# Float64 weights converted a pair of blocks at a time: operations of 512 columns in place of 256

## The chip, the cores and the metric

The kernel runs on one core of one Trainium2 chip. The metric is the device time of one execution in microseconds (us). A core has five engines with queues of their own: TensorE (PE, matrix products), VectorE (DVE), ScalarE (ACT), GpSimd (POOL), and SyncE (SP), which here issues most of the DMAs.

## The reference

A layer that mixes channels in the frequency domain, and two gated MLPs on its result; the weights of the MLPs come as float64, because NumPy's scaling of them made them so.

```python
X = np.fft.rfft(x, axis=1)                  # x: 2 x 3008 x 256, float32
Yr = Xr @ w_r - Xi @ w_i + b_r
Yi = Xr @ w_i + Xi @ w_r + b_i
Yr = np.sign(Yr) * np.maximum(np.abs(Yr) - 0.01, 0.0)      # Yi likewise
y = np.fft.irfft(Y, n=3008, axis=1)
...
h = x @ w_in                                # x: 6016 x 256, w_in: 256 x 2048
x = (h * sigmoid(1.702 * h)) @ w_out        # w_out: 2048 x 256
h = x @ w_in2
out = (h * sigmoid(h)) @ w_out2
```

## The kernel before

The program goes through a forward transform as matrix products (0 to about 77 us), the channel mixing (to about 152 us), the inverse transform (to about 216 us), and the two MLPs. The tokens of an MLP are worked on in six blocks, `i` = 0 to 5, of 1024 tokens (the last has 896). A block has eight groups, `p` = 0 to 7, one for each pair of 128-wide blocks of the hidden width. A group makes the seven products of a Strassen-Winograd scheme with `w_in` (L772), adds them up (L784 on DVE, L794 on ACT), applies the activation (L776), splits its result in an upper and a lower float32 part (L778 on ACT, L780 on DVE or POOL), and multiplies with `w_out` (L744). One group is 45 matmuls. Layer 0 lasts from 216 to about 748 us, layer 1 from there on.

**The conversion.** Each of the 64 blocks of the four weight matrices (two layers, `w_in` and `w_out`, 16 blocks each) is 128 x 256 float64. `cv_load` brings it in by one DMA on SP (L146, 256 KB, tile `raw64`). ACT takes the magnitude of the upper words (L155, tile `cv_c`), and DVE makes five steps: two operations with a constant (L160, L161), one that joins the sign to it (L162, writes `cv_a`), another with a constant (L163), and one that makes the rest of the value from the lower words (L164, writes `cv_c`). `settle` then adds the two parts (L221, by the table `cva` three times in four on POOL and else on DVE). For layer 1, and for the first blocks of `w_out`, the sum is spilled to DRAM (L224) and fetched later; else it is put in place. The five steps are laid into the list `fill`, from which `pump` takes them between the MLP's adds (L785), so that they are spread over DVE's queue.

**Placing.** `place_out` makes the upper part of a block by a copy on ACT (L99) and the lower by a subtraction (L100). `place_in` waits for two blocks, makes four sums of 128 columns from them on DVE (L195, L196, L198, L200), and splits the seven left factors in four pieces: of 256, 128, 256 and 256 columns, each with a copy (L99) and a subtraction (L100, on DVE or POOL by the tables `pil` and `mvl`).

**Buffers.** The pool `cv` has two `raw64` buffers, two `cv_c`, four `cv_a` and two for fetched blocks of `w_out`, each of one block, and one of 512 columns for the sums.

**What sets the order.** Ahead of the MLP, `tick` converts a block after those groups that the tables `tf` (forward), `tm` (mixing) and `ti` (inverse) list, 19 blocks in all; in block 0 the table `kb` gives the blocks converted in each group, 16 in all; after that `kr` = 1 block a group is converted up to the last, which is started at about 609 us. Inside a group, `settle` runs at hook 1 and `window`, which starts the next blocks, at hook 2. A scheduler orders the engines' queues by a simulated timeline, but `region` keeps some of them in the order of the program: POOL and SP in the forward part, SP in the mixing, PE in the inverse, none in block 0 of layer 0, and DVE and SP in its later blocks.

## Time and profile before

| | |
|---|---|
| Three runs | 1244.52, 1243.29, 1242.84 us; median 1243.29 us |
| Span of the profiled execution | 1241.9 us, 1.4 us below that median |
| Busy: PE, DVE, ACT, POOL | 1193.9, 904.3, 709.1, 691.3 us |
| DVE's steps L160 to L164 | 64 of each, 30 of each between 80 and 318 us |

The profiled execution's own time is given by its span alone. Busy times are sums of durations; the durations of neighbouring instructions of DVE overlap a little, so that the distance from start to start is shorter than the duration. A busy PE is not PE at its peak, since matmuls are pipelined and their ends are modelled; the number of matmuls in a stretch says more.

### The profile page before, as it was taken

The page shows a single profiled execution, that of the slowest core. Times are in us where ns is not written, and L with a number is a line of the kernel's source. Part 1 is how long each engine was busy: PE and PEld are TensorE (multiplying, and loading weights), DVE is VectorE, ACT ScalarE, POOL GpSimd, SP SyncE. Part 2 cuts the span into 40 slices and gives each one's busy share as a digit, 9 for nine tenths or more (in the row PEclk, how much of TensorE's full clock was granted, in tenths as well). Part 3 has the DMA queues.
Part 4 walks back from the last instruction along what each step waited for, and adds up shares of the span by engine and source line. Part 5 has one row for each costly group of instructions (what it writes and reads, how often), then busy time and mean ns, then how long its engine had stood idle before and what let it go on. Part 6 is the DMA issues. An engine that isn't in the chain of part 4 may idle for free.

```text
span 1241.9 us, 15776 instructions
## 1 busy us (share of the span) xinstructions
PE 1193.9 (96%) x5220; PEld 969.5 (78%) x5220; DVE 904.3 (73%) x1543; ACT 709.1 (57%) x1393; POOL 691.3 (56%) x579
## 2 busy tenths in 40 slices
PE   7889889799999999999999999999999999999998
PEld 4877679577688787787888977888888888888897
DVE  7899999999967868678758886465564564655654
ACT  3566644656655656556556675565564555554654
POOL 4666655646545647547556575464464554553643
PEclk9889889799999999999999999999999999999999
DMA  8441123111110111111100110000000000000000
GB/s 330 170 160 55 52 73 130 36 52 60 33 44 27 39 39 39 39 39 38 43 18 9 56 39 9 1 35 1 1 34 1 1 35 1 27 8 1 35 1 30
DMA packets 33012, 57.11 MB, mean 46 GB/s; under 512 B 3233, under 2 KB 22689, under 8 KB 31650
## 3 DMA queue, kind: packets, MB, share of 16 engines
q1 hardware_dynamic: 30882, 41.42, 10.3%
q0 software_dynamic: 2048, 14.68, 3.2%
q8 instruction: 41, 0.67, 0.2%
q14 instruction: 41, 0.34, 0.1%
HBM read 44.68 MB, written 11.40 MB: 45 GB/s over the span
## 4 chain that ended last, share of the span: by engine, by line
PE 65%; DVE 7%; issue 2%; ACT 1%; POOL 0%; DMA 0%; DVEq 0%; ACTq 0%
PE o L744 35%; PE x L772 30%; DVE yt L784 3%; DVE cv_s L196 1%; DVE tmp L697 1%; DVE g L780 0%; DVE x L100 0%; ACT yt L776 0%; DMA raw<-in_wo 0%; DVE tmp L691 0%; ACT g L778 0%; ACT wi L99 0%; DVE cv_c L164 0%; ACT x L99 0%; DVE wi L100 0%
## 5 line engine op out<-in xcount | busy, mean ns | idle before, releaser
L784 DVE TENSOR_TENSOR yt<-yt,x 128x512 f32<-128x512 f32 (+1 forms) x672 | 450.9, 673 | 275.2 <-PE x L772 204.8
L780 POOL TENSOR_TENSOR g<-yt,g 128x512 fp32r<-128x512 f32 (+1 forms) x324 | 416.4, 1295 | 418.1 <-ACT g L778 301.2
L744 PE MATMUL o<-g,wo 128*128 128x512 f32 (+1 forms) x2304 | 604.3, 392 | 2.4 <-ACT yt L748 1.1
L772 PE MATMUL x<-x,wi 128*128 128x512 f32 (+1 forms) x2016 | 543.3, 394 | 15.2 <-DVE yt L784 10.8
L744 PEld LDWEIGHTS o<-g,wo 128*128 128x128 f32 x2304 | 432.9, 188 | 101.7 <-ACT g L778 2.8
L772 PEld LDWEIGHTS x<-x,wi 128*128 128x128 f32 x2016 | 378.4, 189 | 108.3 <-DVE yt L784 19.6
L776 ACT ACTIVATE yt<-yt 128x512 f32<-128x512 f32 (+1 forms) x384 | 237.4, 622 | 292.0 <-DVE yt L784 290.0
L778 ACT CAST g<-yt 128x512 fp32r<-128x512 f32 (+1 forms) x384 | 231.9, 609 | 8.6
L780 DVE TENSOR_TENSOR g<-yt,g 128x512 fp32r<-128x512 f32 (+1 forms) x60 | 49.0, 819 | 33.1 <-ACT g L778 33.1
L100 POOL TENSOR_TENSOR x<-yt,x 128x512 fp32r<-128x512 f32 (+1 forms) x41 | 58.5, 1435 | 14.5 <-ACT x L99 12.7
L155 ACT ACTIVATE cv_c<-raw 128x256 f32<-128x256 f32 x64 | 27.8, 438 | 65.6 <-DMA raw<-in_wo 36.6
L794 ACT COPY yt<-x 128x512 f32<-128x512 f32 (+1 forms) x96 | 54.9, 572 | 9.9 <-PE x L772 9.5
L221 POOL TENSOR_TENSOR cv_a<-cv_a,cv_c 128x256 f32<-128x256 f32 x48 | 41.2, 863 | 23.9 <-DVE cv_c L164 21.4
L164 DVE SCALAR_TENSOR_TENSOR cv_c<-raw,cv_c 128x256 f32<-128x256 uint32 x64 | 51.0, 805 | 0.0
L356 PE MATMUL psi<-m,fh 128*128 128x376 f32 (+3 forms) x208 | 48.7, 324 | 0.3 <-ACT rt L623 0.3
L496 PE MATMUL psm<-wc_hi,xtl 128*128 128x512 f32 x96 | 39.3, 413 | 3.3 <-DVE xtl L100 3.3
L356 PE MATMUL psf<-m,xh 128*128 128x376 f32 (+1 forms) x160 | 39.3, 341 | 2.0 <-ACT xh L307 1.2
L496 PE MATMUL psm<-wc_hi,xth 128*128 128x512 f32 x96 | 40.2, 419 | 1.0 <-ACT xth L99 1.0
L356 PE MATMUL psi<-m,fl 128*128 128x376 f32 (+3 forms) x104 | 34.2, 329 | 6.8 <-POOL fl L100 5.0
L496 PE MATMUL psm<-wc_lo,xth 128*128 128x512 f32 x96 | 39.0, 406 | 0.0
L356 PEld LDWEIGHTS psi<-m,fh 128*128 128x128 f32 x208 | 37.1, 196 | 0.5 <-ACT rt L623 0.4
L356 PEld LDWEIGHTS psf<-m,xh 128*128 128x128 f32 x160 | 30.3, 216 | 3.3 <-ACT xh L307 1.7
(111 smaller groups left out, 979.6 us busy)
## 6 DMA issues: line engine op xcount, KB each, us to landing
raw<-in_wi SPq DMA_DIRECT2D x32, 256.0 KB, 2.7
raw<-in_wo SPq DMA_DIRECT2D x32, 256.0 KB, 2.7
raw<-in_x SPq DMA_DIRECT2D x12, 512.0 KB, 4.9
out_t<-yt SPq DMA_DIRECT2D x20, 256.0 KB, 2.0
m<-in_mf POOLq DMA_DIRECT2D x4, 1128.0 KB, 7.9
m<-in_mi POOLq DMA_DIRECT2D x4, 1128.0 KB, 6.2
w_out<-cv_a SPq DMA_DIRECT2D x24, 128.0 KB, 1.7
cv_ld<-w_out SPq DMA_DIRECT2D x24, 128.0 KB, 2.0
```

The source lines that it names most:

```text
L100: (lo_eng or nc.vector).tensor_sub(lo, src, r32(hi))
L164: lambda: stt(out=c, in0=w[:, :, 0], scalar=2.0**-52, in1=c, op0=ALU.mult, op1=ALU.mult),
L221: E('cva', u[2]).tensor_add(a, a, c)
L356: nc.tensor.matmul(ps, a, z, start=i == 0 and x == 0, stop=i == last and x == 2)
L496: nc.tensor.matmul(t, a, w, start=(n == 0), stop=(n == 11 and grp == 1))
L744: nc.tensor.matmul(acc[h, mm], st, mv, start=first and k == 0, stop=last and k == 2)
L772: nc.tensor.matmul(ps, st, mv, start=m == 0, stop=m == 2)
L776: nc.scalar.activation(g, g, func)
L778: nc.scalar.copy(gh, g)
L780: E('gl3' if l else 'gl0' if i == 0 else 'gl2' if i == last else 'gl', ng[0]).tensor_sub(gl, g, r32(gh))
L784: (nc.vector.tensor_sub if sub else nc.vector.tensor_add)(out, u, v)
L794: nc.scalar.copy(ya, p1)
```

## The change

Every list, buffer and step of the conversion goes by pairs of blocks. A pair is loaded as 128 x 512 float64 (512 KB): of `w_out` by one DMA (L149 of the changed kernel), of `w_in` by two of 256 KB (L145, L146), which lay the four pieces in the order that the placing wants. ACT's magnitude (L158), the five steps (L163 to L167) and the add (L218) have 512 columns, and one spill or fetch moves 256 KB. `place_out` is one copy and one subtraction of 512 columns for a pair; `place_in` keeps its four sums of 128 columns and splits in two pieces, of 384 and 512 columns. The MLP's own lines move up by four (L784 is L780, L780 is L776).

The pool has one `raw64` and one `cv_c` buffer, two `cv_a` and one for fetched pairs of `w_out`, each of a pair; their bytes are the same. A pair's load can start when L167 of the pair ahead has read `raw64`, and its magnitude when that pair's add has read `cv_c`. The tables `cva`, `pil` and `mvl` are now read by the number of the pair. Ahead of the MLP nine pairs are converted (three by `tf`, three by `tm`, three by `ti`), in block 0 nine (one a group, and by the new table `kb2` a second one in group 1, at hooks 4 and 5), and one in each of the next 14 groups, those of block 1 and the first six of block 2.

```diff
-CFG = {..., 'tf': [6, 9, 12], 'tm': [2, 3, 4, 5, 7, 14], 'ti': [2, 2, 3, 4, 5, 10, 12, 13, 13, 15, 15], 'kb': [2, 4, 2, 2, 2, 2, 0, 2], ...}
+CFG = {..., 'tf': [6, 9, 12], 'tm': [2, 4, 7], 'ti': [2, 5, 13], 'kb': [1, 1, 1, 1, 1, 1, 1, 1], ...}
...
-            raw = cv_p.tile([P, CU], mybir.dt.int64, tag="raw", name="raw64")
+            raw = cv_p.tile([P, 2 * CU], mybir.dt.int64, tag="raw", name="raw64", bufs=1)
             if kind == "in":
-                src = w[:, c * P : (c + 1) * P].rearrange("(k p) f -> p k f", p=P)
+                r = raw[:, :].rearrange("p (s f) -> p s f", s=4)
+                src = w[:, 2 * p * P : 2 * (p + 1) * P].rearrange("(k p) f -> p k f", p=P)
+                nc.sync.dma_start(out=r[:, 1:3], in_=src[:, :, :P])
+                nc.sync.dma_start(out=r[:, 0:4:3], in_=src[:, :, P:])
             else:
-                src = w[c * P : (c + 1) * P, :]
-            nc.sync.dma_start(out=raw, in_=src)
+                src = w[2 * p * P : 2 * (p + 1) * P, :].rearrange("(r p) d -> p r d", p=P)
+                nc.sync.dma_start(out=raw[:, :].rearrange("p (r d) -> p r d", r=2), in_=src)
...
-        c = cv_p.tile([P, CU], F32, tag="c", name="cv_c")
-        a = cv_p.tile([P, CU], F32, tag="a", name="cv_a", bufs=N("ca"))
+        c = cv_p.tile([P, 2 * CU], F32, tag="c", name="cv_c", bufs=1)
+        a = cv_p.tile([P, 2 * CU], F32, tag="a", name="cv_a")
...
-                lambda: add(t12[:, 0], a1[:, 0], a1[:, 1]),
-                lambda: sub(t34[:, 0], a0[:, 0], a1[:, 0]),
-                lambda: put(slice(0, 2), a0),
-                lambda: sub(t12[:, 1], t12[:, 0], a0[:, 0]),
-                lambda: put(2, a1[:, 1]),
-                lambda: sub(t34[:, 1], a0[:, 1], t12[:, 1]),
-                lambda: put(slice(3, 5), t12),
-                lambda: (put(slice(5, 7), t34), w_in.update({(l, p): w})),
+                lambda: add(t[:, 0], a[:, 0], a[:, 3]),
+                lambda: sub(t[:, 2], a[:, 1], a[:, 0]),
+                lambda: put(slice(0, 3), a[:, 1:4]),
+                lambda: sub(t[:, 1], t[:, 0], a[:, 1]),
+                lambda: sub(t[:, 3], a[:, 2], t[:, 1]),
+                lambda: (put(slice(3, 7), t), w_in.update({(l, p): w})),
...
-        cv_load(2 - len(loaded))
+        cv_load(1 - len(loaded))
...
-        cv_load(max(k - len(loaded), 0))
+        cv_load(max(min(k, 1) - len(loaded), 0))
...
+            if (l, i) == (0, 0) and p in N('kb2'):
+
+                if h == 4:
+                    pump()
+                    cv_load(1 - len(loaded))
+                    second.extend(settle())
+                if h == 5:
+                    window(1, second)
```

DVE's queue in block 0 of layer 0, before. The names are output<-inputs; `x` is a product in PSUM, `yt` the sums, `g` the split activation.

```order
L160 TENSOR_SCALAR cv_c_2941<-cv_c_2941 128x256
L160 TENSOR_SCALAR cv_c_3045<-cv_c_3045 128x256
L784 TENSOR_TENSOR yt_1699<-yt_1699,x_3026 128x512
L784 TENSOR_TENSOR yt_1699<-yt_1699,x_3095 128x512
L161 TENSOR_SCALAR cv_c_2941<-cv_c_2941 128x256
L161 TENSOR_SCALAR cv_c_3045<-cv_c_3045 128x256
L784 TENSOR_TENSOR yt_1699<-yt_1699,x_3091 128x512
L162 SCALAR_TENSOR_TENSOR cv_a_2942<-raw64_2902,cv_c_2941 128x256
L162 SCALAR_TENSOR_TENSOR cv_a_3046<-raw64_3004,cv_c_3045 128x256
L780 TENSOR_TENSOR g_3088<-yt_1699,g_3087 128x512
L163 TENSOR_SCALAR cv_c_2941<-cv_a_2942 128x256
L163 TENSOR_SCALAR cv_c_3045<-cv_a_3046 128x256
```

The same queue and block after the change, with the end of one pair's conversion and the start of the next.

```order
L165 SCALAR_TENSOR_TENSOR cv_a_2817<-raw64_2781,cv_c_2816 128x512
L780 TENSOR_TENSOR yt_1679<-yt_1679,x_2852 128x512
L780 TENSOR_TENSOR yt_1679<-yt_1679,x_2856 128x512
L166 TENSOR_SCALAR cv_c_2816<-cv_a_2817 128x512
L776 TENSOR_TENSOR g_2849<-yt_1679,g_2848 128x512
L167 SCALAR_TENSOR_TENSOR cv_c_2816<-raw64_2781,cv_c_2816 128x512
L780 TENSOR_TENSOR yt_1679<-yt_1679,x_2890 128x512
L776 TENSOR_TENSOR g_2879<-yt_1679,g_2878 128x512
L780 TENSOR_TENSOR yt_1679<-yt_1679,x_2906 128x512
L780 TENSOR_TENSOR yt_1679<-yt_1679,x_2902 128x512
L163 TENSOR_SCALAR cv_c_2919<-cv_c_2919 128x512
```

Before, the steps of two blocks stood next to each other; after, each step stands once, and between the last step of a pair (L167) and the first of the next (L163) there are four rows, in other groups of this block four to nine.

DVE's queue in block 1 of layer 0, where the order is that of the program, before.

```order
L164 SCALAR_TENSOR_TENSOR cv_c_3487<-raw64_3450,cv_c_3487 128x256
L784 TENSOR_TENSOR yt_1699<-yt_1699,x_3552 128x512
L784 TENSOR_TENSOR yt_1699<-yt_1699,x_3570 128x512
L780 TENSOR_TENSOR g_3577<-yt_1699,g_3576 128x512
L784 TENSOR_TENSOR yt_1699<-yt_1699,x_3566 128x512
L160 TENSOR_SCALAR cv_c_3580<-cv_c_3580 128x256
L784 TENSOR_TENSOR yt_1699<-yt_1699,x_3591 128x512
L161 TENSOR_SCALAR cv_c_3580<-cv_c_3580 128x256
```

The same place after.

```order
L167 SCALAR_TENSOR_TENSOR cv_c_3246<-raw64_3208,cv_c_3246 128x512
L780 TENSOR_TENSOR yt_1679<-yt_1679,x_3312 128x512
L780 TENSOR_TENSOR yt_1679<-yt_1679,x_3330 128x512
L776 TENSOR_TENSOR g_3337<-yt_1679,g_3336 128x512
L780 TENSOR_TENSOR yt_1679<-yt_1679,x_3326 128x512
L163 TENSOR_SCALAR cv_c_3340<-cv_c_3340 128x512
L780 TENSOR_TENSOR yt_1679<-yt_1679,x_3351 128x512
L164 TENSOR_SCALAR cv_c_3340<-cv_c_3340 128x512
```

The four rows between one conversion and the next are the same four (three adds and a `g`); the next conversion is now that of a pair.

SP's queue in the same blocks, before.

```order
L146 DMA raw64_3450<-in_wi2 128x2x128
L224 DMA w_in1_3_3463<-cv_a_3383 128x256
L146 DMA raw64_3545<-in_wi2 128x2x128
L224 DMA w_in1_4_3558<-cv_a_3488 128x256
L146 DMA raw64_3638<-in_wi2 128x2x128
L224 DMA w_in1_5_3651<-cv_a_3581 128x256
```

And after.

```order
L145 DMA raw64_3096<-in_wi2 128x2x128
L146 DMA raw64_3096<-in_wi2 128x2x128
L221 DMA w_in1_1_3118<-cv_a_3023 128x512
L145 DMA raw64_3208<-in_wi2 128x2x128
L146 DMA raw64_3208<-in_wi2 128x2x128
L221 DMA w_in1_2_3222<-cv_a_3141 128x512
```

Before, the spill of a block stood between two loads, the load in front of it being that of the block after next; after, two DMAs load a pair, and its `raw64` is the only one.

## Rows read from the trace of the kernel before

**Rows 1.** The page: the span, and the chain of work that ended last, as shares of the span by engine.

```profile
span 1241.9 us, 15776 instructions
...
PE 65%; DVE 7%; issue 2%; ACT 1%; POOL 0%; DMA 0%; DVEq 0%; ACTq 0%
```

**Rows 2.** Busy time of each engine in stretches of 20 us, with the granted clock of TensorE (PEclk, as a share of 2.4 GHz) and the DMA share. The columns are the stretch, then busy us and instructions of PE, its weight loads (PEld), DVE, ACT and POOL.

```profile
20.00:40.00 20.00, 18.60 (x97) 16.29 (x96) 17.02 (x48) 10.16 (x44) 11.15 (x7) 1.00 0.72 270
...
80.00:100.00 20.00, 20.00 (x82) 14.72 (x81) 19.97 (x43) 14.53 (x31) 11.78 (x12) 1.00 0.15 50
...
140.00:160.00 20.00, 16.71 (x55) 12.26 (x54) 20.00 (x39) 9.68 (x17) 12.74 (x12) 0.74 0.19 59
160.00:180.00 20.00, 14.03 (x88) 13.21 (x87) 19.93 (x38) 10.70 (x22) 11.08 (x10) 0.86 0.13 41
180.00:200.00 20.00, 19.74 (x129) 19.57 (x128) 20.00 (x34) 6.81 (x14) 14.07 (x15) 0.97 0.67 245
...
220.00:240.00 20.00, 13.78 (x38) 9.43 (x39) 19.86 (x37) 11.14 (x22) 15.66 (x15) 0.66 0.10 33
...
320.00:340.00 20.00, 20.00 (x87) 16.10 (x86) 17.29 (x30) 13.10 (x25) 9.65 (x10) 1.00 0.15 46
```

**Rows 3.** The chain of work that ended last, in order of time, where it changes engines: start, us, what.

```profile
316.93 1.72 DVE g L780
...
318.69 1.20 PE o L744 x4
```

**Rows 4.** Timeline of PE between 125 and 330 us, two of the matmuls before which it stood idle: start, us, the group, and in brackets the idle time and what ended it.

```profile
148.36 0.80 PE L496 MATMUL psm<-wc_hi,xtl 128*128 128x512 f32 x1 [3.29 <-DVE xtl L100]
...
175.27 0.68 PE L356 MATMUL psi<-m,fl 128*128 128x378 f32 x1 [4.99 <-POOL fl L100]
```

**Rows 5.** Groups of DVE's conversion steps between 80 and 216 us (channel mixing and inverse transform): busy us, mean ns of one, idle before.

```profile
L163 DVE TENSOR_SCALAR cv_c<-cv_a 128x256 uint32<-128x256 uint32 x15 | 7.5, 506 | 0.0
L162 DVE SCALAR_TENSOR_TENSOR cv_a<-raw,cv_c 128x256 uint32<-128x256 uint32 x15 | 7.4, 503 | 0.0
L160 DVE TENSOR_SCALAR cv_c<-cv_c 128x256 f32<-128x256 f32 x17 | 6.6, 395 | 0.0
L164 DVE SCALAR_TENSOR_TENSOR cv_c<-raw,cv_c 128x256 f32<-128x256 uint32 x15 | 6.2, 425 | 0.0
L161 DVE TENSOR_SCALAR cv_c<-cv_c 128x256 uint32<-128x256 uint32 x17 | 4.8, 294 | 0.0
```

**Rows 6.** The same view of DVE between 216 and 320 us (block 0 of layer 0): the MLP's adds (L784), the last conversion step (L164) and the adds of the two halves of a weight (L221).

```profile
L784 DVE TENSOR_TENSOR yt<-yt,x 128x512 f32<-128x512 f32 x57 | 37.9, 676 | 0.2
...
L164 DVE SCALAR_TENSOR_TENSOR cv_c<-raw,cv_c 128x256 f32<-128x256 uint32 x15 | 9.8, 666 | 0.0
...
L221 DVE TENSOR_TENSOR cv_a<-cv_a,cv_c 128x256 f32<-128x256 f32 x4 | 3.4, 858 | 0.0
```

**Rows 7.** All instructions on the conversion's tile cv_c in the whole run: duration in ns as min/median/max, first and last start.

```profile
L160 DVE TENSOR_SCALAR cv_c<-cv_c x64: 273/284/1373, 35.6 to 619.8; 128x256 f32<-128x256 f32 x64
L161 DVE TENSOR_SCALAR cv_c<-cv_c x64: 274/283/792, 36.7 to 620.7; 128x256 uint32<-128x256 uint32 x64
L162 DVE SCALAR_TENSOR_TENSOR cv_a<-raw,cv_c x64: 404/415/956, 37.1 to 621.5; 128x256 uint32<-128x256 uint32 x64
L163 DVE TENSOR_SCALAR cv_c<-cv_a x64: 274/285/1399, 38.1 to 622.5; 128x256 uint32<-128x256 uint32 x64
L164 DVE SCALAR_TENSOR_TENSOR cv_c<-raw,cv_c x64: 409/473/1535, 43.9 to 624.7; 128x256 f32<-128x256 uint32 x64
```

**Rows 8.** Timeline of DVE in block 0: start, us, the group. Two blocks' steps stand next to each other here (x2).

```profile
290.75 0.48 DVE L161 TENSOR_SCALAR cv_c<-cv_c 128x256 uint32<-128x256 uint32 x2
291.16 0.68 DVE L784 TENSOR_TENSOR yt<-yt,x 128x512 f32<-128x512 f32 x1
291.75 0.75 DVE L162 SCALAR_TENSOR_TENSOR cv_a<-raw,cv_c 128x256 uint32<-128x256 uint32 x2
292.42 0.68 DVE L780 TENSOR_TENSOR g<-yt,g 128x512 fp32r<-128x512 f32 x1
```

**Rows 9.** The one operation of the program that has one input, a constant, and 512 columns, on DVE (L334): ns as min/median/max.

```profile
L334 DVE TENSOR_SCALAR wc_lo<-wc_lo x1: 407/407/407, 67.6 to 67.6; 128x512 fp32r<-128x512 f32 x1
```

**Rows 10.** DMA issues on SP's queue: KB each, and median us from issue to landing.

```profile
raw<-in_wi SPq DMA_DIRECT2D x32, 256.0 KB, 2.7
...
raw<-in_x SPq DMA_DIRECT2D x12, 512.0 KB, 4.9
...
wc_f<-in_wc SPq DMA_DIRECT2D x1, 512.0 KB, 3.4
```

**Rows 11.** Timeline of all engines in block 1 of layer 0, the steps between one converted block and the next: start, us, engine, the group, idle time before.

```profile
433.16 1.30 DVE L164 SCALAR_TENSOR_TENSOR cv_c<-raw,cv_c 128x256 f32<-128x256 uint32 x1
...
435.72 0.38 SPq L146 DMA_DIRECT2D raw<-in_wi  x1
...
438.15 1.48 DVE L784 TENSOR_TENSOR yt<-yt,x 128x512 f32<-128x512 f32 x2 [2.33 <-PE x L772]
438.44 0.44 ACT L155 ACTIVATE cv_c<-raw 128x256 f32<-128x256 f32 x1 [1.24 <-DMA raw<-in_wi]
...
439.55 0.28 DVE L160 TENSOR_SCALAR cv_c<-cv_c 128x256 f32<-128x256 f32 x1
```

**Rows 12.** Busy time in a stretch of 50 us of blocks 1 and 2, columns as in Rows 2.

```profile
400.00:450.00 50.00, 49.06 (x206) 37.96 (x205) 39.47 (x64) 28.73 (x53) 28.61 (x23) 1.00 0.13 40
```

67 lines of the change are left out of this document (30 added, 37 removed).

## The prediction

> **What bounds the kernel now.** I read the shares of the chain first, then the chain in order of time, then busy times stretch by stretch, and then the stretches in which an engine is short. By its shares the chain is TensorE's: PE 65%, DVE 7% [rows 1]. The order of time corrects this: up to 318.6 us the chain runs through DVE, from 318.7 us on through PE's matmuls [rows 3]. The stretches agree. From 80 to 320 us DVE is busy 19.9 of 20 us, while PE loses 6.0 us of 160 to 180 and 6.2 us of 220 to 240, with its granted clock down to 0.74, 0.86 and 0.66 in the three worst stretches [rows 2], after it stood waiting for splits from DVE and POOL, 3.29 and 4.99 us the longest times [rows 4]. So work taken from DVE between 80 and 318 us is worth time where PE is short of work, and after 320 us (87 matmuls in 20 us, DVE no longer full [rows 2]) it is worth nothing. Even inside the first part PE is full in two stretches: 82 matmuls between 80 and 100, and 19.74 us busy between 180 and 200 [rows 2].
>
> Of the conversion, thirty of the 64 blocks lie in the stretch bound by DVE (five before it, 29 after it).
>
> **The change, part by part.** All terms are in us on the span (1241.9), which lies 1.4 below the median of the runs; I add them to the median, 1243.3.
>
> A. *Five steps of 512 columns for ten of 256, fifteen times.* The removed instructions cost less than their durations, because the next one starts before the one ahead ends: two L161 take 0.41 us from start to next start, two L162 0.67, an add of 512 columns 0.59, though its duration is 0.68 [rows 8]. The operation with a constant takes 0.407 at 512 columns [rows 9], less the same 0.07 of overlap 0.34. Two blocks without disturbance are then 2 x (3 x 0.205 + 2 x 0.335) = 2.57, and a pair 3 x 0.34 + 2 x 0.59 = 2.20: 0.4 saved, 0.08 an instruction removed.
> But the steps don't run undisturbed. Between 80 and 216 us their means are 0.395, 0.294, 0.503, 0.506 and 0.425, together 2.12 us a block [rows 5], the shortest of the run 0.273, 0.274, 0.404, 0.274 and 0.409, together 1.63 [rows 7]. The excess is 0.49 a block, 0.98 for two; between 216 and 320 it is 0.26 a block in L164 alone (0.666 [rows 6] against 0.409). It is time that an instruction waits for another engine, most likely POOL. Were it paid per instruction, half the instructions would pay half: of a mean of 0.75 for two blocks 0.37 would go. Were it paid per column, nothing of it would go. I take three quarters of 0.37, since the excess falls unevenly on the steps (L163 almost doubles, L161 hardly grows [rows 5]), as single collisions do: 0.4 + 0.28 = 0.68 a pair, with 0.4 and 0.4 + 0.98 as ends. Fifteen pairs: **-10.2** (-6 to -20).
> There is a rule that speaks against the 0.28. The Trainium skill, "SBUF — State Buffer", section "Who interferes with whom", says that a DVE instruction with two SBUF inputs contends with GpSimd's reads of SBUF, and that of two instructions that want the shared pair of ports the first holds it for its whole length while the other stands still. By that a POOL add of twice the columns holds DVE twice as long, and the 0.28 would be 0. The trace has L164, with two inputs, at 0.409 to 1.535, as the rule would have it, but also L163, which has one input, at 0.274 to 1.399 [rows 7]; no row shows what a longer POOL add does.
>
> B. *Adds and placing.* Four of the eight pairs of layer 0 have their lower parts subtracted on DVE, two operations fewer each; four of DVE's eight adds of L221 in the stretch go, the others growing to twice the size. Twelve instructions at 0.08: **-1.0** (-3 if the adds, at a mean of 0.858 [rows 6] four times as dear as their columns, lose their excess too; 0 at worst).
>
> C. *One block more is converted before the MLP's block 1* (36 against 35). The three pairs of the forward part in place of its blocks fall where DVE has some idle time (busy 17.0 of 20 us), but PE is short there too (18.6 of 20) [rows 2]. One block, 0.2 x 3 + 0.34 x 2: **+1.3** (0 to 1.6).
>
> D. *One buffer in place of two, in block 0.* In this term and in E, L163 and L167 are lines of the changed kernel, the first and the last step. After L167 of a pair the load of the next must be issued, land, and ACT must take its magnitude, before DVE can go on with L163. DVE works in order: an L163 that waits holds the adds of the MLP behind it, and PE and ACT wait for these. Before, the load of the block after next was long under way. The time from end to start, in parts: a second issue of 0.38 us [rows 11]; a landing of 512 KB, which the trace shows as 3.4 us (one load of the mixing's weights) and 4.9 (the loads of x at the start), where 256 KB takes 2.7 [rows 10]; I take 3.4, since the loads of weights meet little other traffic (a DMA share of 0.10 to 0.19 in most stretches from 80 us on, 0.72 where x is loaded [rows 2]). ACT at most doubles its 0.44 [rows 11]. Together 4.7. Of DVE's rows between L167 and the next L163 the order of the changed kernel has nine, five, nine, six, four, seven, five and four in block 0; at 0.68 a row (L784's mean [rows 6]) these are 6.1, 3.4, 6.1, 4.1, 2.7, 4.8, 3.4 and 2.7 us. What lacks is 1.3 + 0.6 + 2.0 + 1.3 + 2.0 = 7.2. Some of these rows themselves wait for PE and fill the gap: in block 1 four rows took 5.1 us, from the end of a block's last step at 434.46 to the next one's first at 439.55, a wait of 2.33 for PE among them [rows 11]. I take **+4.5** (0 to 7.2).
>
> E. *A pair in each of 14 groups of blocks 1 and 2* in place of a block. There PE bounds: DVE is busy 39.5 of 50 us [rows 12], which leaves 2.2 in a group of 10.5. A pair costs 0.9 more than a block (2.20 less half of 2.57). The 4.7 fit in the 5.1 of the four rows that stand there still. A tenth a group: **+1.5** (0 to 7). If the cover of 5.1 goes, because the wait for PE in it goes, the other 1.3 of slack is next, so a stall up to that is free.
>
> F. ACT's magnitudes, the spills and fetches, the loads' issues on SP: nothing. ACT is busy 9.7 to 14.5 of 20 us in the stretch [rows 2], and SP's queue holds only DMAs, spaced by the conversion. The last pair is converted in block 2, before the last block of layer 0 takes the weights up, as before.
>
> The sum is -10.2 - 1.0 + 1.3 + 4.5 + 1.5 = -3.9: a span of 1238.0, **1239.4** on the scale of the median; its own range is 1236 to 1242. The lost clock is not in it: it could only add to the gain.
>
> **The rivals.**
> *Slower: loads that land late.* If 512 KB lands in 4.9 us as the loads of x did [rows 10], the chain of D is 6.2. In block 0 the rows lack 16.3 us instead of 7.2, in the proportion of D 10.2; in the 14 groups 1.1 over the 5.1, of which half stays after the slack: 7.5. The sum is -10.2 - 1.0 + 1.3 + 10.2 + 7.5 = +7.8, 1251. Between landings of 3.4 and 4.9 us D and E together grow from 6.0 to 17.7, so from about 4.2 us this one decides. For it: the only repeated loads of 512 KB are the slow ones. Against: these ran beside a DMA share of 0.72 [rows 2], which the weights don't meet, and a pair of `w_in` goes as two of 256 KB. Chance 0.22.
> *No change: PE is full where the time is saved.* If half of A falls in stretches like 80 to 100 and 180 to 200 [rows 2], A is -5.1 and the sum +1.2: 1244.5. For it: the mixing holds many of the conversions. Against: a DVE that runs ahead shortens the later waits of PE. Chance 0.08.
> *No change: the excess stays.* Contention paid per column: A is 15 x 0.4 = 6.0, the sum +0.3: 1243.6. This is what the rule of the Trainium skill named under A makes of it. For it L164's excess, against it L163's. Chance 0.08.
> *More: the single buffer costs nothing.* The scheduler laid L163 where its own timeline had the load done; if that holds, D and E are 0, and with the half of the excess A is 15 x 0.77 = 11.6: -11.3, 1232. Part of the lost clock could come on top. Chance 0.16.
>
> **How the numbers follow.** The forecast has 0.46, of which 0.38 lies under 1240.8. About 0.2%, or 2.5 us, is what a measurement of this kernel tells from no change. Faster: 0.38 + 0.16 = 0.54. Same: 0.08 + 0.08 + 0.08 = 0.24. Slower: 0.22. The range of 1231 to 1250 leaves out the upper half of the slow rival (0.11) and a part of the fast one (0.05).
>
> **What would show it.** A: the five steps of a pair should have a sum of means near 2.58 + half of 0.98, about 3.1 us between 80 and 216; at 3.5 the excess stayed. PE's losses between 140 and 180 us should shrink, and the end of DVE's part in the chain move from 318.7 to about 315. D: waits of DVE at L163 (of the changed kernel, as below) for ACT's magnitude, and of that for the load, some 0.5 us a group in block 0; the landing of a pair near 3.4. E: DVE's waits in blocks 1 and 2 without a wait of PE for an add. I am wrong if L163 stands for 1 us or more a group, or if PE, after 320 us, starts to wait for L780.

## The result, and the profile after

The changed kernel takes 1258.45 us (median of four runs, 1257.3 to 1260.75) against 1243.9 for the kernel before: 1.0114 times as long, 95% interval 1.0093 to 1.0136. It is 14.5 us slower, where 3.9 less was forecast. One execution of a kernel below (h2_all_late) took 1312.64 us at a mean granted clock of 0.844 and is left out of its median. The profiled execution of the changed kernel has a span of 1258.8 us, 16.9 above that of before.

The page of the changed kernel: span, busy times, and the shares of the chain.

```profile
span 1258.8 us, 15280 instructions
...
PE 1197.1 (95%) x5220; PEld 966.2 (77%) x5220; DVE 874.6 (69%) x1337; ACT 697.0 (55%) x1313; POOL 694.5 (55%) x545
...
PE 59%; DVE 3%; issue 3%; ACT 2%; POOL 1%; DMA 0%; DVEq 0%; POOLq 0%; ACTq 0%; SPq 0%
```

DVE does less than before (874.6 us in 1337 instructions, against 904.3), as the change means it to, and PE is busy for the same time. PE's share of the chain is smaller than it was [rows 1].

Busy times of the changed kernel in stretches of 20 us, columns as in [rows 2].

```profile
60.00:80.00 20.00, 14.07 (x80) 12.52 (x80) 18.25 (x30) 12.76 (x45) 13.12 (x11) 0.79 0.59 195
80.00:100.00 20.00, 19.72 (x78) 14.31 (x78) 19.46 (x32) 10.46 (x19) 11.66 (x10) 0.95 0.34 106
...
140.00:160.00 20.00, 16.27 (x59) 11.59 (x58) 19.91 (x29) 9.25 (x16) 10.59 (x10) 0.91 0.12 40
160.00:180.00 20.00, 13.70 (x90) 12.79 (x89) 16.69 (x29) 12.79 (x24) 12.30 (x10) 0.85 0.19 53
180.00:200.00 20.00, 19.34 (x110) 18.84 (x111) 20.00 (x31) 5.01 (x11) 9.67 (x12) 0.81 0.51 177
...
220.00:240.00 20.00, 12.86 (x47) 9.47 (x46) 19.45 (x30) 9.27 (x17) 13.25 (x11) 0.72 0.09 26
...
320.00:340.00 20.00, 16.78 (x64) 12.46 (x63) 19.13 (x27) 11.49 (x22) 10.81 (x8) 0.91 0.12 39
340.00:360.00 20.00, 20.00 (x87) 15.98 (x86) 15.82 (x27) 10.82 (x19) 11.12 (x9) 1.00 0.25 79
```

Each stage ends later: DVE is still full from 320 to 340 us, where before it had fallen to 17.29 [rows 2], and 64 matmuls fit there in place of 87. But from 160 to 180 us DVE is less full than it was: 16.69 us, where it had been 19.93. It has less to do, stands idle for longer there, and the kernel is later. That is not what a kernel bound by DVE's work alone would show. PE's losses between 140 and 180 us, which the prediction had shrink, went from 9.3 us [rows 2] to 10.0.

The conversion's steps between 85 and 223 us (mixing and inverse) in the changed kernel, to be held against [rows 5].

```profile
L164 DVE TENSOR_SCALAR cv_c<-cv_c 128x512 uint32<-128x512 uint32 x8 | 6.6, 822 | 0.2
L167 DVE SCALAR_TENSOR_TENSOR cv_c<-raw,cv_c 128x512 f32<-128x512 uint32 x7 | 5.4, 770 | 0.1
L165 DVE SCALAR_TENSOR_TENSOR cv_a<-raw,cv_c 128x512 uint32<-128x512 uint32 x7 | 4.8, 685 | 0.1
...
L166 DVE TENSOR_SCALAR cv_c<-cv_a 128x512 uint32<-128x512 uint32 x7 | 3.5, 502 | 0.0
L163 DVE TENSOR_SCALAR cv_c<-cv_c 128x512 f32<-128x512 f32 x7 | 2.9, 417 | 0.1
```

Their means add up to 3.20 us a pair, where two blocks took 4.25. The prediction gave 3.1 if part of the excess went and 3.5 if none did. So the saving on DVE itself is there, and about as forecast.

**Where the time is lost.** PE's matmuls are the same 5220 in both kernels, so one can ask of each trace at what time the nth of them starts (n from 0, the start times of PE's matmuls in order). Columns are n, the place, the time in the kernel before, and how much later the others are, all in us; "no steps", h4_all and h5 (h5_not_at_change) are experiments told below.

```
   n  place                        before   after   before,no steps   after,no steps   h4_all   h5
 280  end of forward part            74.2    -3.7        -3.5              -7.0          +0.9    0.0
 320  start of mixing                84.6    +3.3        -0.3              -2.5          +0.9   +0.1
 500  mixing                        128.8    +3.3        -0.3              -2.1          +0.9   +0.1
 700  inverse transform             183.3    +5.2       -15.3             -18.3          -2.8   -2.4
 897  end of inverse                215.9    +7.0       -11.6             -12.9          +1.5   -0.1
1300  first group of block 1        329.1   +10.2       -14.1             -14.8          +7.1   +5.5
1500  sixth group of block 1        375.7   +11.0       -14.1             -14.8          +7.1   +5.5
1700  block 2                       424.7   +17.6       -15.9             -17.0          +6.8   +3.2
2600  block 4                       637.4   +14.8       -17.5             -19.7          +8.4   +0.4
5219  last                         1237.4   +16.7       -19.6             -18.7          +7.7   -0.7
```

Five places lose: the start of the mixing 3.3 us (7.0 from n = 280 to 320, where the forward part had been ahead), the inverse 3.7, block 0 of layer 0 3.2, blocks 1 and 2 7.4, of which 2.8 come back by n = 2600, when the kernel before still converts a block in each group; and the end of layer 0 with the start of layer 1 1.9.

### The profile page after: what moved, and what is told of

Same layout as the page of the kernel before. It is cut to its first block, busy times and chain, and to the rows that moved or that the text cites. A ratio compares the mean times of both kernels' runs of the same rounds, so it can differ in the third digit from the quotient of the medians.

```text
span 1258.8 us, 15280 instructions
## 1 busy us (share of the span) xinstructions
PE 1197.1 (95%) x5220; PEld 966.2 (77%) x5220; DVE 874.6 (69%) x1337; ACT 697.0 (55%) x1313; POOL 694.5 (55%) x545
## 4 chain that ended last, share of the span: by engine, by line
PE 59%; DVE 3%; issue 3%; ACT 2%; POOL 1%; DMA 0%; DVEq 0%; POOLq 0%; ACTq 0%; SPq 0%
PE o L740 32%; PE x L768 27%; DVE yt L780 2%; ACT yt L772 1%; POOL g L776 1%; DVE cv_s L196 1%; ACT g L774 1%; DMA raw<-in_wo 0%; POOL x L100 0%; ACT wi L99 0%; ACT yt L790 0%; DVE yt L744 0%; ACT x L99 0%; DVE x L100 0%; DVE tmp L693 0%
## 5 line engine op out<-in xcount | busy, mean ns | idle before, releaser
L780 DVE TENSOR_TENSOR yt<-yt,x 128x512 f32<-128x512 f32 (+1 forms) x672 | 451.0, 673 | 289.2 <-PE x L768 209.2
L776 POOL TENSOR_TENSOR g<-yt,g 128x512 fp32r<-128x512 f32 (+1 forms) x324 | 423.3, 1318 | 401.7 <-ACT g L774 297.6
L776 DVE TENSOR_TENSOR g<-yt,g 128x512 fp32r<-128x512 f32 (+1 forms) x60 | 52.1, 869 | 44.1 <-ACT g L774 44.0
L100 POOL TENSOR_TENSOR x<-yt,x 128x512 fp32r<-128x512 f32 (+1 forms) x41 | 58.0, 1422 | 17.9 <-ACT x L99 16.4
L218 POOL TENSOR_TENSOR cv_a<-cv_a,cv_c 128x512 f32<-128x512 f32 x24 | 34.0, 1415 | 33.3 <-DVE cv_c L167 26.8
L352 PE MATMUL psf<-m,xh 128*128 128x376 f32 (+1 forms) x160 | 36.2, 324 | 3.0 <-ACT xh L299 3.0
L158 ACT ACTIVATE cv_c<-raw 128x512 f32<-128x512 f32 x32 | 21.4, 669 | 30.2 <-DMA raw<-in_wi 14.8
L509 ACT ACTIVATE th<-sd,neglam 128x512 f32<-128x512 f32 x24 | 16.4, 716 | 25.5 <-DVE sd L504 19.7
```

The lines of the kernel that those rows point to most:

```text
L100: (lo_eng or nc.vector).tensor_sub(lo, src, r32(hi))
L158: nc.scalar.activation(c, hf, AF.Abs, scale=2.0**-112)
L218: E('cva', u[2]).tensor_add(a, a, c)
L352: nc.tensor.matmul(ps, a, z, start=i == 0 and x == 0, stop=i == last and x == 2)
L776: E('gl3' if l else 'gl0' if i == 0 else 'gl2' if i == last else 'gl', ng[0]).tensor_sub(gl, g, r32(gh))
L780: (nc.vector.tensor_sub if sub else nc.vector.tensor_add)(out, u, v)
```

## Experiments

Differences of a few us are read from the medians of four or more runs, with the ratio to the kernel before, and their place from the list above. The changed kernel, e1_spread and e2_spread_early run the same instructions in the same order up to 344 us, and their lists still differ there: +7.0, +5.8 and +5.4 at n = 897, +10.2, +9.0 and +8.7 at n = 1300. A difference of 1.5 us between two lists says little. Line numbers are those of the changed kernel, in runs on the kernel before those of that kernel.

### Is it the steps, or all the rest?

The five steps are left out of either kernel, and the add takes the magnitude twice, so that the weights are not the right ones; loads, magnitudes, adds, spills and placing stay.

```diff
-        fill.extend(
-            (
-                lambda: ts(c, c, C_HI, None, op0=ALU.min),
...
-        )
         return a, c
...
-            E('cva', u[2]).tensor_add(a, a, c)
+            E('cva', u[2]).tensor_add(a, c, c)
```

Expected of the kernel before without steps:

> The kernel before with the five DVE steps of the conversion left out (the add takes the magnitude twice, so the weights are not the right ones); loads, magnitudes, adds, placing, spills and their times stay. It gives the whole price of the steps of 256 columns. If DVE bounds the stretch from 80 to 320 us, as I read the profile, thirty blocks of some 1.7 us there are 50 us of DVE's work, and 15 us or more of the span should go, until PE bounds it (PE lacks some 32 us there in idle time and clock). If it is rather the chain of waits between DVE, POOL and ACT that bounds it, under 8 us go.

and of the changed one:

> The changed kernel with its five steps left out in the same way. The difference to the run before this one is the price of all the rest of the change: loads by pairs, single buffers, adds and placing of larger pieces, other times of conversion. If the steps and their density make the loss, the two are within 3 us of each other. If the rest makes it, the changed kernel stays 8 us or more behind even without steps.

Measured: 1226.9 us (ratio 0.9850, 0.9828 to 0.9871) and 1226.03 (0.9840, 0.9817 to 0.9864). They are level, to 1 us. Loads by pairs, single buffers, larger adds and placing, other places in the program cost nothing, taken together, as long as the steps are away. With the steps the one takes 17.7 us more (1244.63 in the same session) and the other 32.4. Up to n = 1300 the steps of the kernel before are worth 14.1 us, those of the changed kernel 10.2 and 14.8, 25.0.

The run on the kernel before says something about the prediction's ground, too. Its busy times in the two stretches, columns as in [rows 2]:

```profile
80.00:216.00 136.00, 125.93 (x618) 104.43 (x617) 124.27 (x187) 80.23 (x154) 83.09 (x77) 0.99 0.23 77
216.00:320.00 104.00, 98.58 (x403) 76.69 (x403) 83.74 (x125) 65.50 (x135) 55.75 (x55) 0.97 0.17 51
```

With all ten steps of two blocks gone, thirty blocks or 49 us of DVE at the undisturbed 1.63 a block [rows 7], the 1300th matmul came 14.1 us earlier (the steps of the first five blocks, gone as well, gave 0.3 by n = 320). So a microsecond taken from DVE there is worth 0.29 on the path, not 1. This is the mean over all that was taken away; the first microseconds can be worth another amount. Between 80 and 216 us DVE remains busy 124 of 136 us and PE 126: both are nearly full.

### Are steps of 512 columns themselves bad?

Each step is made as two operations of 256 columns, nothing else is changed.

```diff
-                lambda: ts(c, c, C_HI, None, op0=ALU.min),
+                lambda f=f: [f(slice(h * CU, (h + 1) * CU)) for h in range(2)]
+                for f in (
+                    lambda s: ts(c[:, s], c[:, s], C_HI, None, op0=ALU.min),
...
```

> The changed kernel with each of the five DVE steps of a pair made as two operations of 256 columns, one behind the other: the size of the operations alone is undone, loads, buffers, adds, placing and times of conversion stay. If the larger steps save what the trace says in block 0 (0.79 us a pair against before), eight pairs there and part of those ahead lose it again: 3 to 8 us slower, 1261 to 1266. If steps of 512 columns are themselves what hurts (they hold POOL longer), it gets faster by 2 us or more.

Measured: 1274.91 us (1.0247, 1.0227 to 1.0268), 16.5 slower than the changed kernel. So the operations of 512 columns are good in this structure, and better than forecast, but not where they were forecast: at n = 1300 this run is where the changed kernel is (+10.5, against +10.2), although the five steps that start between n = 320 and n = 1300 take some 67 us of DVE in all, instead of 46 (durations, added up). Nearly the whole loss comes in blocks 1 and 2 (+30.2 at n = 2600, against +14.8), in whose groups PE alone bounds when the steps are away. The last step there, in the changed kernel and in this one (L169), between 330 and 490 us: mean ns of one.

```profile
L167 DVE SCALAR_TENSOR_TENSOR cv_c<-raw,cv_c 128x512 f32<-128x512 uint32 x14 | 17.4, 1242 | 0.0
```

```profile
L169 DVE SCALAR_TENSOR_TENSOR cv_c<-raw,cv_c 128x256 f32<-128x256 uint32 x26 | 27.8, 1107 | 0.0
```

Two of 1107 ns stand for one of 1242. What halving costs where conversions are less dense is h6_all_half, below.

### Does the length of POOL's operations matter?

> The changed kernel with the add of the two parts of a pair (24 on POOL at 1.3 us, 8 on DVE) made as two of 256 columns. If one POOL operation of 1.3 us standing in DVE's way is what costs in the forward and mixing parts, two of 0.74 let DVE in between: 2 to 4 us faster there, the 500th matmul at 130 us or earlier instead of 132.1. If the length of the add is not the matter, no change beyond 1.5 us, or slightly slower for the added operations.

```diff
-            E('cva', u[2]).tensor_add(a, a, c)
+            for h in range(2):
+                s = slice(h * CU, (h + 1) * CU)
+                E('cva', u[2]).tensor_add(a[:, s], a[:, s], c[:, s])
```

Measured: 1259.84 us (1.0124, 1.0105 to 1.0142), n = 500 at 133.3. Nothing came back: the length of the add alone is not the matter.

> The changed kernel with the placing of w_in in four pieces of 256, 128, 256 and 256 columns as before, in place of 384 and 512. If long operations of POOL and of ACT's queue in the placing hold up DVE and PE ahead of the MLP, 2 us or more come back. If not, the eight pairs of layer 0 pay two more operations each on ACT, DVE and POOL, and it is 0 to 2 us slower.

```diff
-                lambda: put(slice(0, 3), a[:, 1:4]),
+                lambda: put(slice(0, 2), a[:, 1:3]),
                 lambda: sub(t[:, 1], t[:, 0], a[:, 1]),
+                lambda: put(2, a[:, 3]),
                 lambda: sub(t[:, 3], a[:, 2], t[:, 1]),
-                lambda: (put(slice(3, 7), t), w_in.update({(l, p): w})),
+                lambda: put(slice(3, 5), t[:, 0:2]),
+                lambda: (put(slice(5, 7), t[:, 2:4]), w_in.update({(l, p): w})),
```

Measured: 1259.04 us (1.0110, 1.0090 to 1.0130): nothing either.

### Density, and the one buffer

```diff
-        k = 0 if l == 1 or i == last else N('kb')[p] if i == 0 else N('kr')
+        k = 0 if l == 1 or i == last else N('kb')[p] if i == 0 else (p + 1) % 2
```

> The changed kernel, but after block 0 a pair is converted in every second group only (14 pairs over blocks 1 to 4) instead of in each of 14 groups in a row. The changed kernel reaches its 1500th matmul 11.0 us late and its 1700th 17.6 us late, and has 14.8 left at the 2600th. If it is the density of conversions that cost this (a pair's 2.6 us of DVE and 1.3 of POOL in each group, and in the change of blocks near 415 us), some 4 to 6 us come back: 1253 to 1255. If it is the single buffer (DVE waits at L163 for a load that starts too late, 12.4 us in 14 times), each pair still pays its wait, only in other groups, and the time stays within 2 us of 1258.5.

And with this, an earlier load:

```diff
-        cv_load(max(min(k, 1) - len(loaded), 0))
+        cv_load(0 if l == 1 or i == last else 1 - len(loaded))
```

> As the run before this one, but a pair's load is issued at the start of the group ahead of its conversion, as soon as the one buffer is free, so that it has landed a group before the first step. By the theory of density it changes nothing against the run before (DVE had slack there); by the theory of the single buffer the waits at L163, 12.4 us in blocks 1 and 2, go and the time falls by 3 us or more against the run before.

Measured: 1256.58 (1.0098, 1.0075 to 1.0122) and 1255.27 (1.0085, 1.0068 to 1.0101), by the medians 1.9 and 3.2 us less than the changed kernel; the first lies within the 2 us that I had left to the single buffer. The lists show more: from n = 1300 to 1700 the changed kernel loses 7.4 us against the kernel before, these two win 0.4 and 0.1; from n = 1300 to 2600 the three lose 4.6, 1.1 and 1.3. So the spread gives back some 3.5 us in these blocks. DVE's waits between 330 and 490 us in the changed kernel (total us, times, longest):

```profile
DVE cv_c L163 <- ACT cv_c L158: 12.4, 9, 2.2
DVE g L776 <- ACT g L774: 11.5, 7, 2.8
```

and what DVE's instructions on the conversion's tile waited for the same magnitude on ACT, in the whole run of e1_spread (total us, times):

```profile
  ACT cv_c L158: 1.0, 3
```

My expectation was ill made: these waits go when the conversions are spread, without an earlier load, since the buffer is then long free. So the two runs don't tell density from the one buffer: a pair a group, loaded only when the pair ahead lets go, is both. Starting the load earlier on top is worth nothing that can be measured.

**Time of each group.** The same list, read from n = 897 on in steps of 45 matmuls, is the time of each group, us. A group that PE alone bounds takes 10.5. The eighth number (before the bar) holds the change from block 0 to block 1, the first of each later block the change ahead of it.

```
                  block 0                                       | block 1                                 | block 2 (first 3)
before            22.4 10.5 12.0 10.5 11.3 10.8 10.7 14.9       | 10.5 10.5 10.5 10.5 10.5 10.5 10.5 10.5 | 12.8 10.5 10.5
after             22.2 12.7 12.5 10.5 10.7 11.2 10.5 15.7       | 10.9 10.5 10.5 10.5 11.3 10.6 11.7 12.2 | 16.4 10.5 10.5
after, half steps 20.9 13.1 13.0 10.5 10.5 12.5 11.8 16.2       | 11.4 11.4 11.8 10.9 12.7 11.8 14.4 12.0 | 17.6 10.8 11.2
before, no steps  20.5 14.9 12.8 10.5 10.5 10.5 10.5 10.5       | 10.5 10.5 10.5 10.5 10.5 10.5 10.5 10.5 | 11.0 10.5 10.5
e1_spread         22.1 12.8 12.4 10.5 10.7 11.2 10.5 15.7       | 10.9 10.5 10.5 10.5 10.5 10.5 10.5 10.5 | 12.4 10.5 10.5
h5                22.1 11.6 13.3 10.5 12.3 10.9 10.6 17.3       | 10.5 10.5 10.5 10.5 10.5 10.5 10.5 10.5 | 10.5 10.5 10.5
```

Here the places stand out. In an ordinary group a block, or a pair in every second group, costs nothing. Pairs in every group cost 3.8 us in the last four groups of block 1 (11.3, 10.6, 11.7 and 12.2, where e1_spread has 10.5 each). At the change of blocks, where the next tokens are prepared on DVE, ACT and POOL, a group takes 12.8 with a block and 16.4 with a pair in a row of pairs, 11.0 and (in the changed kernel) 10.6 without steps. The 7.4 us that blocks 1 and 2 lose are these two places, about half each: 3.8, and 16.4 against 12.8.

### The start of the mixing

SP's queue in the changed kernel between 44 and 65 us: start, us, the issue.

```profile
44.70 0.38 SPq L145 DMA_DIRECT2D raw<-in_wi  x1
...
63.19 0.37 SPq L145 DMA_DIRECT2D raw<-in_wi  x1
...
64.11 0.47 SPq L323 DMA_DIRECT2D wc_f<-in_wc  x1
```

The load of the mixing's weights (L323) goes out at 64.11 us, behind the third pair's load, which waits in SP's queue for the one buffer. In the kernel before:

```profile
49.07 0.34 SPq L327 DMA_DIRECT2D wc_f<-in_wc  x1
```

Then DVE and POOL in the changed kernel, 66 to 72 us:

```profile
66.27 1.30 POOL L218 TENSOR_TENSOR cv_a<-cv_a,cv_c 128x512 f32<-128x512 f32 x1
...
66.51 5.19 DVE L314 TENSOR_TENSOR xl<-dd,xh 128x256 fp32r<-128x256 f32 x1 [1.37 <-ACT xh L303]
...
67.53 1.02 POOL L100 TENSOR_TENSOR wi<-cv_a,wi 128x384 fp32r<-128x384 f32 x1
...
68.50 1.27 POOL L100 TENSOR_TENSOR wi<-tmp,wi 128x512 fp32r<-128x512 f32 x1
...
69.74 0.72 POOL L314 TENSOR_TENSOR xl<-dd,xh 128x256 fp32r<-128x256 f32 x1
70.42 1.00 POOL L100 TENSOR_TENSOR wi<-cv_a,wi 128x384 fp32r<-128x384 f32 x1
...
71.76 1.00 PE L352 MATMUL psf<-m,xl 128*128 128x376 f32 x2 [0.47 <-DVE xl L314]
```

A subtraction of 256 columns takes DVE 5.19 us, while POOL runs the second pair's add, three pieces of the placing of the first two pairs and a subtraction of the forward part, one behind the other; PE waits for it. Last, ACT's queue and PE's first matmul of the mixing:

```profile
74.28 0.62 ACT L99 CAST wi<-tmp 128x512 fp32r<-128x512 f32 x1 [3.60 <-DVE tmp L199]
74.81 1.04 ACT L99 CAST wc_hi<-wc_f 128x1024 fp32r<-128x1024 f32 x1
...
77.81 0.79 PE L492 MATMUL psm<-wc_hi,xth 128*128 128x512 f32 x1 [4.12 <-ACT xth L99]
```

and that matmul in the kernel before:

```profile
76.80 0.50 PE L496 MATMUL psm<-wc_hi,xth 128*128 128x512 f32 x1 [1.03 <-ACT xth L99]
```

ACT stands 3.60 us for a sum of the second pair's placing (L199), has the weights to copy next, which came late, and the first split of the mixing waits behind them: PE stands 4.12 us, where it stood 1.03 before. Even so the mixing starts only 1.0 us later than before. Most of the rest of the 3.3 at n = 320 is the clock: in the changed kernel TensorE was granted 1.2 GHz in the first microseconds of the mixing, in the kernel before 2.4. The stretch in both, the changed kernel first, columns as in [rows 2]:

```profile
77.00:82.00 5.00, 3.90 (x9) 2.56 (x9) 5.00 (x11) 4.42 (x11) 2.81 (x4) 0.50 0.23 61
```

```profile
77.00:82.00 5.00, 5.00 (x23) 4.09 (x23) 4.97 (x5) 4.61 (x14) 4.66 (x5) 1.00 0.76 285
```

Five runs looked at these waits.

```diff
-CFG = {... 'tf': [6, 9, 12], 'tm': [2, 4, 7], ...}
+CFG = {... 'tf': [6, 9], 'tm': [1, 2, 4, 7], ...}
```

> The changed kernel with the third of the forward part's conversions moved into the channel mixing (after its groups 1, 2, 4 and 7 in place of 2, 4 and 7). In the changed kernel PE stands 4.1 us before the mixing's first matmul for a copy on ACT, ahead of which ACT had stood 3.6 us for a sum of the placing of a pair. If that place is what costs 3.3 us at the start of the mixing, they come back there: the 320th matmul at 85 us instead of 87.9, and 2 to 4 us at the end. If DVE's load bounds instead, the mixing pays the same later: no change at the end.

Measured: 1259.07 us (1.0120, 1.0092 to 1.0148), n = 320 at 88.4. Missed.

```diff
-        if g == 10:
+        if g == 8:
             load_wc()
```

> The changed kernel with the load of the mixing's weights (wc_f) issued on SP ahead of the third pair's load instead of behind it. In the kernel before it was issued at 49.1 us, in the changed one at 64.1, because the load in front of it waited for the one raw buffer to come free. If that wait in SP's queue costs the 3.3 us at the start of the mixing, the load goes out near 50 us, the 320th matmul at 85 us instead of 87.9, and 2 to 4 us come back at the end. If it is the work of a third pair on DVE and ACT there, the start of the mixing stays at +3 against the kernel before.

Measured: 1258.05 us (1.0119, 1.0101 to 1.0138). The load went out at 48.39 us, but n = 320 came at 87.8. Missed as well; the profiled run is 4.2 us ahead of the changed kernel's at n = 897, the median is not. Then the other way round, in the kernel before, whose `load_wc()` is moved behind the tick of group 12:

> The kernel before with the load of the mixing's weights issued behind the next block's load, as it stands in the changed kernel. By the theory of SP's queue it goes out some 11 us later, near 60 us, and 2 to 4 us are lost at the start of the mixing; if the late load has cover there, under 1 us is lost.

The issue on SP there, then PE, DVE and POOL at the start of the mixing:

```profile
45.10 15.74 SPq L146 DMA_DIRECT2D raw<-in_wi  x3
60.89 0.46 SPq L327 DMA_DIRECT2D wc_f<-in_wc  x1
```

```profile
73.47 0.50 PE L496 MATMUL psm<-wc_hi,xth 128*128 128x512 f32 x1 [1.03 <-ACT xth L99]
...
76.13 5.05 DVE L195 TENSOR_TENSOR tmp<-cv_a 128x128 f32<-128x128 f32 x1 [0.61 <-POOL cv_a L221]
...
77.32 3.70 POOL L100 TENSOR_TENSOR xtl<-xt,xth 128x512 fp32r<-128x512 f32 x3
...
82.76 0.79 PE L496 MATMUL psm<-wc_hi,xtl 128*128 128x512 f32 x1 [8.08 <-DVE xtl L100]
```

Measured: 1255.98 us (1.0102, 1.0085 to 1.0120): 13 us lost, 6.8 of them at n = 320, 11.0 at the end of the profiled run, by an edit that issues one DMA of 512 KB 11.8 us later. But PE did not wait for the late weights: it began the mixing at 73.47 us, earlier than the 76.80 of the kernel before. What it stood for, 8.08 us, was a split on DVE, behind a sum of 128 columns of a placing that took 5.05 us beside POOL's operations and 0.28 undisturbed. The edit had changed the order of the instructions on ACT, PE, DVE and POOL, from 58 to 66 us on. So the run shows how dear a changed order can be, and not that a late load of the weights costs 13 us.

> The changed kernel with the load of the mixing's weights ahead of the third pair's (as in g1_weights_first) and with the third conversion taken out of the forward part (after groups 6 and 9 only; in the mixing after 2, 4, 7 and 9), so that no pair's placing stands in ACT's queue between the forward part's last copies and the mixing's first splits more than before. If late weights and the third pair were two causes of which each is enough, the 320th matmul comes at 84 to 86 us (84.6 before, 87.8 with the weights early alone, 88.4 with the third pair later alone). If it comes at 87.5 or later, neither is the cause and it is the steps of the pairs themselves.

```diff
-CFG = {... 'tf': [6, 9, 12], 'tm': [2, 4, 7], ...}
+CFG = {... 'tf': [6, 9], 'tm': [2, 4, 7, 9], ...}
```

Measured, with the weights early: 1261.33 us (1.0135, 1.0107 to 1.0164), n = 320 at 92.2. By its own expectation, 87.5 or later, neither of the two is the cause.

> As g1_weights_first, with the lower parts of layer 0's pairs subtracted on POOL and DVE in turn, as they were before, where the changed kernel has the first two pairs on POOL and the next two on DVE. In the changed kernel a subtraction of 128x256 on DVE at 66.5 us took 5.19 us while POOL ran five operations back to back, the pair's add and placing among them. If such trains of POOL operations are what holds DVE at the start of the mixing, the 320th matmul moves from 87.8 to 86 us or earlier; if not, it stays within 1 us.

```diff
-CFG = {... 'pil': 'PPVV', ...}
+CFG = {... 'pil': 'PVPV', ...}
```

Measured, with the weights early: 1264.25 us (1.0162, 1.0139 to 1.0186), n = 320 at 89.2.

### Places put together

> As the run before this one, and with the pairs after block 0 in every second group, which alone gave 4.7 us in the profile. If the two losses are independent of each other, 6 to 9 us of the 15 come back: 1250 to 1253. What is left then lies in the inverse transform and block 0.

Measured: 1255.59 us (1.0099, 1.0080 to 1.0118): what the spread gives alone, not the sum.

> As g2_both, with the inverse transform's conversions after its steps 5, 8 and 13 in place of 2, 5 and 13, so that no pair is converted where the mixing goes over into the inverse (160 to 180 us, PE waiting for splits and its granted clock at 0.5 from 174 to 188 us in the changed kernel, from 174 to 181 before). If the pair's steps in that stretch are what costs, 2 to 4 us more come back there. If DVE's sum of work counts, the later place costs the same.

Measured, with `'ti': [5, 8, 13]`: 1256.06 us (1.0112, 1.0085 to 1.0138). No change.

> As h1_two_forward, with the pairs after block 0 in every second group and the layer 1 placing of w_in subtracted on DVE as before. Expected is the sum of what these give apart, 5 to 6 us, on top of h1_two_forward: 1250 to 1253, and level with the kernel before (1243) only if the early stages have come back as well.

Measured: 1255.85 us (median of three runs; 1.0099, 1.0078 to 1.0120), which is no more than the spread gives. Missed.

> All edits together: weights of the mixing first, two conversions in the forward part, POOL and DVE in turn, every second group after block 0, layer 1's placing on DVE. If the loss was in where the conversions stand and not in operations of 512 columns, it comes within 4 us of the kernel before or below it (1239 to 1247). If operations of 512 columns beside the other work are themselves the loss, it stays at 1250 or more.

Measured: 1251.44 us (1.0066, 1.0048 to 1.0084). All five edits together, early weights, two conversions in the forward part, POOL and DVE in turn, every second group, layer 1's placing on DVE, bring n = 320 to 85.5 and the end of the inverse to 217.3, 0.9 and 1.5 behind the kernel before. The early ones one or two at a time had given nothing or were slower. By its expectation a time of 1250 or more speaks for the operations of 512 columns themselves; h6_all_half below, in which smaller ones are slower still, speaks against that.

```diff
-        k = 0 if l == 1 or i == last else N('kb')[p] if i == 0 else (p + 1) % 2
+        k = 0 if l == 1 or i == last else N('kb')[p] if i == 0 else int(p in (1, 2, 4, 5))
```

> As h4_all, but no pair is started in the last group of block 0, nor in the first or last of the blocks after it: in these blocks in groups 1, 2, 4 and 5. If a pair's steps at the change of blocks are what costs the last 5 us of block 0 and the 1 to 2 at the changes after it, the 1300th matmul comes some 4 us earlier than in h4_all (336.1) and the time is 1245 to 1248. If the loss stays in block 0's other groups, it is within 1.5 us of 1251.4.

Measured, with `kb` 0 in block 0's last group: 1244.39 us, median of ten runs, 1244.65 for the kernel before beside it: ratio 1.0000, 0.9986 to 1.0013. Of the stretches at the changes of blocks, those of the changed kernel first, columns as in [rows 2]:

```profile
320.00:330.00 10.00, 6.94 (x23) 4.99 (x22) 9.90 (x14) 5.71 (x12) 7.02 (x5) 0.83 0.02 3
...
420.00:430.00 10.00, 7.36 (x25) 3.99 (x24) 7.77 (x12) 4.21 (x8) 7.54 (x5) 1.00 0.20 77
```

and of this run:

```profile
310.00:320.00 10.00, 5.58 (x22) 3.60 (x20) 9.17 (x10) 3.41 (x7) 5.93 (x4) 0.99 0.22 72
320.00:330.00 10.00, 9.84 (x36) 7.89 (x37) 7.55 (x11) 6.11 (x12) 3.88 (x3) 0.83 0.00 0
410.00:420.00 10.00, 10.00 (x45) 8.04 (x44) 7.91 (x12) 6.43 (x12) 7.63 (x7) 1.00 0.00 0
420.00:430.00 10.00, 10.00 (x45) 8.03 (x44) 7.45 (x12) 4.69 (x8) 7.60 (x6) 1.00 0.22 72
```

At the change from block 1 to 2 (near 420 us) PE holds 45 matmuls in 10 us instead of 25. At the end of block 0 nothing was won: that group takes 17.3 us even without a new pair, where without steps it takes 10.5, and n = 1300 is 1.6 earlier than in h4_all instead of 4, which it was already at n = 897, ahead of the edit. What this run has over h4_all it won at the later changes, 6.8 us, and 6.2 against the kernel before, which converts a block at each of the first.

> As h4_all, with each of the five steps made as two operations of 256 columns. In the dense groups of the changed kernel halving cost 15 us, in the stages ahead of 330 us nothing. If operations of 512 columns save DVE time that matters where it bounds (block 0 here), this is 2 to 6 us slower than h4_all; if their gain exists only where conversions are dense, it is within 1.5 us of it.

Measured: 1258.81 us (1.0115, 1.0089 to 1.0141), 7.4 slower than h4_all by the medians and 6 by the ratios to the kernel before (the two were run on different chips); 3.2 of it are there at n = 1300.

## Why the prediction was wrong

**The landing, and the slower rival.** I took 3.4 us for a pair and gave the slower rival a landing of 4.9. DMA issues of the changed kernel:

```profile
raw<-in_wi SPq DMA_DIRECT2D x32, 256.0 KB, 3.1
raw<-in_wo SPq DMA_DIRECT2D x16, 512.0 KB, 3.6
```

3.1 and 3.6: the landing was forecast right. The slower rival had the sign of the result, but its cause, a landing of 4.9, did not come.

**A, the steps, -10.2, the first step that failed.** As DVE's own time it was right (3.20 us a pair, 3.1 forecast). Its worth was not: I let a microsecond of DVE between 80 and 318 us be a microsecond of the end. The steps left out of the kernel before show 0.29 on the mean (14.1 us by n = 1300 for 49), so that 10.2 would have been 3. Halving the steps bears this out: some 21 us more of DVE made 0.3 us at n = 1300 in the changed kernel, some 13 us made 3.2 in h4_all. The chain of waits runs through DVE, as [rows 3] had it; that it also runs through waits that DVE's work doesn't set, and through PE's own work, is my explanation and not shown by itself. The rival that had half of A fall where PE is full came nearest to this worth, and was still too high. What operations of 512 columns save in the changed structure lies mostly after 330 us, where I gave none.

**D, one buffer in block 0, +4.5.** DVE's wait at L163 there was 0.6 us in all, in two waits (in the whole run 13.0 us), and from 60 to 223 us it did not wait there. The term was too large: the rival in which the single buffer costs nothing had this part right.

**E, a pair in each of 14 groups, +1.5.** Too small. Measured 4.6 net (from +10.2 at n = 1300 to +14.8 at n = 2600; +17.6 between them), of which the spread gives some 3.5 back. The waits at L163 that I had put at a tenth of a us a group were 12.4 us in nine places, 0.9 a group over the 14 and near the 1 us that was my sign of being wrong. And I costed an average group: the loss stands in the last four groups of block 1 and in the change of blocks.

**C and F, the other step that failed.** C gave 1.3 for a block more ahead of block 1, F nothing for the issues on SP and ACT's copies. I counted how much work moves, and gave the new places of the conversions no price. Up to n = 1300 the changed kernel loses 10.2 us, where A to D had it win 5.4. Neither the size of the steps makes this loss (halving them moves it by 0.3) nor the rest of the change by itself (without steps the two kernels are level); it is there only with steps at their new places, which cost 25.0 us instead of 14.1. With other places, orders and engines for the same operations of 512 columns the end of the inverse came to +1.5 (h4_all) and -0.1 (h5) instead of +7.0. Who stands behind whom is seen at the start of the mixing: ACT's first split behind a placing that waits for DVE, DVE beside a train of POOL's. The rows of the queues at the border of two stages are where to look for this, and I read them only in block 1.

**The excess and the rule.** By the Trainium skill, "SBUF — State Buffer", section "Who interferes with whom", the one that issues first holds the shared pair of ports for its whole instruction and the other stands still; one rival had the excess stay by it. The same section counts `tensor_scalar` among the operations that can take both pairs of ports, so the excess of L163 of the kernel before need not speak against the rule, as I had it. By means of durations, of seven or eight instructions each, the excess over the shortest of the run fell from 0.98 a pair to 0.62 between 85 and 223 us (3.20 less 2.58, the sum of 0.408, 0.407, 0.677, 0.412 and 0.678). POOL's add in two halves did not help (e4_half_add). The rule's picture, one stands still while the other goes through, does show in the 5.19 us above, there for five operations of POOL in a row. What it costs on the path is not settled: in g4_before_late such an operation of 5.05 us held PE up, but the run meant to break up the train (h3_alternate) was slower.

**What stays open.** In the early stages the edits don't add up: one or two at a time they give nothing or lose up to 6 us, together they give back 2.4 us at the start of the mixing and 5.5 by the end of the inverse. A changed order of one queue moves everything behind it in a program that a scheduler lays out, so I can't say which of the waits is the cause there, nor how much of the loss is the clock that follows them. In blocks 1 and 2 density and the one buffer were not told apart: no run gave a second buffer to a pair in each group. Nor is it settled what makes the last group of block 0 take 14 to 19 us in all kernels with steps; h4_all and h5 still lose 5.6 us in block 0.

## What to carry to other kernels

An engine that is busy 99% of a stretch is not proof that its work sets the end: leave the work out once, and see what a microsecond of it is worth (here 0.29 on the mean) before a saving is priced at 1.

A change in the size of the pieces of background work moves where they stand; look at the borders of stages and blocks, and at every queue the pieces pass, for what comes behind them. Operations of the same size were 14.5 us slower than the old kernel at the first places, 8 us with five edits to their places and engines (h4_all), and level once in addition none was started at a change of blocks (h5).
